# Attention products with v: low part beside the high part, column 0 apart, and two joined block pairs in each head

## The chip, the cores and the metric

The kernel runs on one core of one Trainium2 chip. The time is device microseconds of one execution; 967.84 us is the median of three runs before the change (967.84 to 968.23). The engines are named as in the profile: PE is TensorE (PEld its weight loads), DVE is VectorE, ACT is ScalarE, POOL is GpSimd, SP is SyncE, which here only issues DMAs. Each takes its instructions strictly in the order in which the program issued them to it.

## The reference

Attention in which a query sees the keys of its own hash bucket only, followed by a two-layer feed-forward stage, all in float32:

```
q_bits = (einsum('bhsd,dk->bhsk', q, proj) > 0); k_bits likewise; bucket = sum(bits * 2**k)
scores = where(q_bucket == k_bucket, q k^T / sqrt(64), -1e9)
attn = exp(scores - max); attn /= sum(attn) + 1e-9
x = (attn @ v) laid out as 3072 tokens x 512
h = x @ w_in;  g = (h + 1)^2 / 4 between -1 and 1, h above, 0 below;  out = g @ w_out
```

q, k and v are 4 batches x 8 heads x 768 positions x 64; w_in is 512 x 2048 and w_out 2048 x 512.

## The kernel before

Both stages keep float32 accuracy with TensorE's float32r type, which holds a number with fewer bits: every operand is split into a high part (the rounded number) and a low part (the rest), and a product is the sum of high x high, low x high and high x low.

**Attention** takes about the first 450 us. The 32 heads lie in 16 pairs. A head is cut into 12 units: two halves of 384 queries, and six blocks of 128 keys in each. Unit g (`s_unit`) makes the scores of its block with two matmuls (L421, L422) into one of four PSUM banks `s`; ScalarE takes the exponential twice, once rounded into `ph` (L430) and once in full (L435), back into the bank or, for the units that GpSimd serves, into an SBUF tile `pf`. `lo_unit` of the unit before subtracts the two into `pl` (line 39, the helper `sub`): on GpSimd for blocks 0 and 3 (`POOL_J`), on VectorE for the rest. Four units later (`LAG`), `pv_unit` multiplies with v in three matmuls: `va` x `ph` (L454), `vb` x `ph` (L456) and `va` x `pl` (L458). `va` holds the 64 columns of v's high part and 64 columns of ones, so that the lower or upper half of the 128 output rows collects the sums of the exponentials; `vb` holds v's low part and zeros. The blocks of a half are taken in the order 1, 2, 0, 4, 5, 3 (`PV_ORDER`). After the last, ScalarE copies the bank (L464), and after the second half SP stores the head's result and its sums.

The maxima of head hd + 2 are made meanwhile: after every second unit two matmuls (`max_mm`, L343) fill the one two-bank buffer `smax`, and at the start of the next unit VectorE reduces it (`max_red`, L360). The next two matmuls into `smax` wait for that reduction.

The order of the work is written out by hand. The main loop at the end of `attention` runs over g: scores of unit g, the reduction, `lo_unit(g - 1)`, `pv_unit(g - 4)`, the matmuls for a maximum, and then the tasks entered for that g with `at`. Among these tasks are, for each pair, on even heads: the splitting of the pair after next on GpSimd (`cast_h`, `low_h`), its hash bits (matmuls L219, ScalarE L225, VectorE L230, in units 5 to 8), the cast of the next pair's v on ScalarE (L305, entered for unit 6) and its low part on GpSimd. In most heads, units 9 to 14 carry a share of the conversion of the feed-forward weights from 64-bit words (ScalarE L66, VectorE L70, L74, L78).

**The feed-forward stage** takes the rest. It loads x (the attention result, kept in DRAM as `x_d`), divides it by the sums (`XMaker`) and multiplies with the two weight matrices. GpSimd does nothing in it.

## Time and profile before

| | us |
|---|---|
| median of three runs | 967.84 |
| the profiled execution: span from first to last instruction | 965.5 |
| busy in the span: TensorE, VectorE, ScalarE, GpSimd | 957.1, 752.7, 679.8, 322.7 |
| the pair of heads 18 and 19, from the first scores of one to those of the next | 26.98 |

The span is 2.3 us short of the median; what lies around the first and the last instruction is in the runs' times and not in the span. Matmuls are pipelined, so that the row of one lasts longer than the step from its start to the next start; for a price, the steps are what counts. In the timeline a row gives the start, the duration, engine, line, operation, tiles, shapes and count; in brackets stands how long the engine idled before it and what ended that. Successive operations of VectorE and ScalarE overlap by about a tenth of a microsecond.

### The profile page before, as it was taken

To read this page: it belongs to the slowest core of one execution; us is meant where nothing else is said; L and a number is where in the kernel's file an instruction comes from. 1 tells how busy PE (TensorE), PEld (TensorE's weight loads), DVE (VectorE), ACT (ScalarE), POOL (GpSimd) and SP (SyncE) were. 2 spreads that over 40 slices of the span, in tenths; PEclk is the share of its full clock that TensorE was granted. 3 is DMA by queue.
4 is the path that set the end of the run, shared out by engine and by line. 5 is a ranking of instruction groups with operands and counts; after the bars stand their busy time and mean duration, and the time that the engine had idled before them with its cause. 6 is when DMAs were issued, how large, how long until landed. Compare 5 with 4: busy or idle time off the path is not lost.

```text
span 965.5 us, 15605 instructions
## 1 busy us (share of the span) xinstructions
PE 957.1 (99%) x5050; PEld 889.9 (92%) x5050; DVE 752.7 (78%) x1341; ACT 679.8 (70%) x1481; POOL 322.7 (33%) x435
## 2 busy tenths in 40 slices
...
GB/s 163 189 178 181 164 169 174 183 180 198 202 180 188 158 174 167 148 107 170 186 344 44 200 214 310 308 216 184 120 186 215 156 175 120 147 150 119 121 88 65
DMA packets 95112, 167.55 MB, mean 174 GB/s; under 512 B 13956, under 2 KB 51960, under 8 KB 95032
## 3 DMA queue, kind: packets, MB, share of 16 engines
...
q10 hardware_dynamic: 264, 0.03, 0.0%
...
## 4 chain that ended last, share of the span: by engine, by line
PE 97%; DVE 2%; ACT 1%; issue 0%; DVEq 0%
PE y L893 27%; PE h L1125 18%; PE h L1030 7%; PE s L421 7%; PE o L458 7%; PE o L456 7%; PE o L454 7%; PE s L422 7%; PE smax L343 6%; PE o L219 2%; PE half L343 1%; DVE nm L350 0%; PE half L475 0%; DVE nm L323 0%; PE s L398 0%
## 5 line engine op out<-in xcount | busy, mean ns | idle before, releaser
L430 ACT ACTIVATE ph<-s 128x384 fp32r<-128x384 f32 x380 | 189.8, 500 | 32.1 <-PE s L422 26.1
L360 DVE TENSOR_REDUCE nm<-smax 128x1 f32<-128x768 f32 x168 | 159.9, 952 | 17.5 <-PE smax L343 17.5
L39 DVE TENSOR_TENSOR pl<-s,ph 128x384 fp32r<-128x384 f32 x256 | 137.9, 550 | 26.9 <-ACT s L435 25.6
L39 POOL TENSOR_TENSOR pl<-pf,ph 128x384 fp32r<-128x384 f32 x128 | 129.8, 1014 | 84.3 <-ACT pf L435 79.4
L858 DVE SCALAR_TENSOR_TENSOR t<-t 128x384 f32<-128x384 f32 x128 | 71.3, 557 | 106.7 <-ACT z L853 106.5
L421 PE MATMUL s<-t 128*128 128x384 f32 x384 | 130.5, 340 | 0.0
L454 PE MATMUL o<-ph,va 128*128 128x386 f32 x384 | 130.0, 339 | 0.0
L456 PE MATMUL o<-ph,vb 128*128 128x386 f32 x384 | 130.0, 338 | 0.0
L458 PE MATMUL o<-pl,va 128*128 128x386 f32 x384 | 130.0, 338 | 0.0
L422 PE MATMUL s<-t 128*128 128x384 f32 x384 | 129.4, 337 | 0.0
L435 ACT ACTIVATE s<-s 128x384 f32<-128x384 f32 x252 | 126.2, 501 | 0.0
L893 PE MATMUL y<-t,ghi 128*128 128x512 f32 x384 | 124.6, 395 | 0.0
L852 ACT ACTIVATE t<-h,mh 128x384 f32<-128x384 f32 x56 | 32.5, 581 | 83.7 <-PE h L1030 44.1
L343 PE MATMUL smax<-t 128*128 128x384 f32 x336 | 87.6, 342 | 0.4 <-DVE nm L360 0.3
L863 ACT CAST ghi<-z 128x384 fp32r<-128x384 f32 x129 | 65.2, 505 | 30.1 <-DVE z L859 26.3
L853 ACT ACTIVATE z<-t,m 128x384 f32<-128x384 f32 x128 | 79.0, 617 | 4.2
L893 PEld LDWEIGHTS y<-t,ghi 128*128 128x128 f32 x384 | 71.3, 188 | 11.0 <-ACT ghi L863 0.3
L1125 PE MATMUL h<-wbig,t 128*128 128x384 f32 x399 | 81.4, 336 | 0.0
L852 ACT ACTIVATE t<-wsq,mh 128x384 f32<-128x384 f32 x48 | 29.6, 617 | 67.0 <-DVE wsq L1138 40.8
L1125 PEld LDWEIGHTS h<-wbig,t 128*128 128x128 f32 x399 | 71.6, 188 | 5.2
L893 PE MATMUL y<-t,glo 128*128 128x512 f32 x192 | 76.0, 396 | 0.0
L893 PE MATMUL y<-woh,glo 128*128 128x512 f32 x192 | 75.7, 394 | 0.2
...
## 6 DMA issues: line engine op xcount, KB each, us to landing
...
```

Source lines behind the costliest of these rows:

```text
L39: eng.tensor_tensor(out=out, in0=a, in1=b, op=ALU.subtract)
L343: nc.tensor.matmul(out=ps[:, 0:HS], lhsT=t2[:, 0, h, i * P:(i + 1) * P], rhs=t2[:, 1, h, hf * HS:(hf + 1) * HS], start=True, stop=True)
L360: nc.vector.tensor_reduce(out=nmp(hd)[:, i:i + 1], in_=smax[hd][:, :, 0:HS], axis=AX.XY, op=ALU.max, negate=True)
L421: nc.tensor.matmul(out=ps[:, 0:HS], lhsT=t1[:, 1, h, ks], rhs=t1[:, 0, h, sl], start=True, stop=False)
L422: nc.tensor.matmul(out=ps[:, 0:HS], lhsT=t2[:, 1, h, ks], rhs=t2[:, 0, h, sl], start=False, stop=True)
L430: nc.scalar.activation(out=ph[:, 0:HS], in_=ps[:, 0:HS], func=AF.Exp, scale=SCALE)
L435: nc.scalar.activation(out=pf, in_=ps[:, 0:HS], func=AF.Exp, scale=SCALE)
L454: nc.tensor.matmul(out=o, lhsT=wa, rhs=ph, start=(jj == 0), stop=False)
L456: nc.tensor.matmul(out=o, lhsT=wb, rhs=ph, start=False, stop=False)
L458: nc.tensor.matmul(out=o, lhsT=wa, rhs=pl, start=False, stop=(jj == NJ - 1))
L893: nc.tensor.matmul(out=ys[c][m], lhsT=g_[:, m * P:(m + 1) * P], rhs=w, start=(first and k == 0), stop=(last and k == 2))
L1125: nc.tensor.matmul(out=ps, lhsT=w[:, cs], rhs=x, start=(n == 0 and s not in (2, 3, 6)), stop=(n == 5), skip_group_check=True)
```

## The change

- One tile `VT` replaces `va` and `vb`: for each key block and head 64 columns of v's high part and beside them the low part of columns 1 to 63, with a column of ones in place of the low part's column 0. One matmul with `ph` and one with `pl` then give the high product in rows 0 to 63 and the low product in rows 65 to 127, with the sums in row 64.
- The low part of v's column 0 is left. It has a table of its own, `v0lo`, for all heads, and a matmul of one output row with `ph`, added to row 0. The tables come from a new input `v0` in two loads, and `first_column` makes them: for the first three pairs ahead of the first cast, for the rest at unit 40. `cast_v` gets a second copy that places the high part of column 0.
- From head 4 on (`FROM` = 48) the column-0 products of blocks 4 and 5 of a head's first half (unit 5) and of blocks 0 and 1 of its second half (unit 7) are joined: `z_unit` makes z = ratio x `ph` of the unit before + the full exponential of this unit on VectorE, and one matmul with the later block's `v0lo` serves both. The ratios are made once (`ratios`); `z_ends` sets two columns for each pair from pair 2 on. A joined product is issued up to three units later than the others.
- `QUARTER_J` gives GpSimd one more low part, that of block 1 in the second half of odd heads (from unit 48 to head 29). `pf` gets a third buffer.
- A head's result is stored as two tensors, `x_d` and the low product `l_d`; `add_low` adds the second to the first by accumulating DMAs from GpSimd's queue, two for each batch.
- Products with `pl`, and all products of a first half, are 384 columns wide, not 386. The memsets of `vb` and of the ends of `pl` fall away.

```diff
+FROM = 48
 POOL_J = (0, 3)
+QUARTER_J = ((0, 3), (0, 3), (0, 3), (0, 1, 3))
...
     def cast_v(pr, eng):
-        (eng.copy if eng is nc.scalar else eng.tensor_copy)(out=VA[pr % NV][:, :, 0::2], in_=vraws[pr])
+        copy = eng.copy if eng is nc.scalar else eng.tensor_copy
+        vt = VT[pr % NV]
+        copy(out=vt[:, :, 0::2, 1:], in_=vraws[pr][:, :, :, 1:])
+        copy(out=vt[:, :, 0::2, 0], in_=v0hi[:, pr].bitcast(F32))
...
+    def first_column(a, b, eng):
+
+        n = slice(2 * NJ * a, 2 * NJ * b)
+        hi, lo = (x.rearrange("p a j h -> p (a j h)")[:, n] for x in (v0hi, v0lo))
+        t = v0_raw[:, n]
+        if eng is nc.gpsimd:
+            eng.tensor_scalar(out=hi, in0=t, scalar1=AWAY, scalar2=0.0, op0=ALU.mult, op1=ALU.add)
...
+        sub(nc, eng, t, t, hi.bitcast(F32))
+        eng.tensor_scalar(out=lo, in0=t, scalar1=0.0, scalar2=TINY, op0=ALU.is_equal, op1=ALU.mult)
+        eng.tensor_tensor(out=lo, in0=lo.bitcast(F32), in1=t, op=ALU.add)
...
     def pool_lo(g):
-        return g % NJ in POOL_J
+        return g % NJ in (QUARTER_J[g // NJ % 4] if FROM <= g < (NH - 2) * NU else POOL_J)
...
+    def z_ends(pr):
+
+        nc.vector.tensor_scalar(out=ZT[0][:, :, HS:HS + 2],
+                                in0=ratio[:, pr, 0].rearrange("p (h o) -> p h o", o=1).to_broadcast([P, 2, 2]),
+                                scalar1=1.0, scalar2=None, op0=ALU.add)
+
+    def z_unit(g):
+
+        hd, n = g // NU, g % NJ // 4
+        if g not in zpair:
+            return
+        pa, pb = units[g - 1][1], units[g][0]
+        zs[g] = ZT[n][:, hd % 2]
+        nc.vector.scalar_tensor_tensor(out=zs[g][:, 0:HS], in0=pa[:, 0:HS].bitcast(F32),
+                                       scalar=ratio[:, hd // 2, n, hd % 2:hd % 2 + 1],
+                                       in1=pb, op0=ALU.mult, op1=ALU.add)
...
-        _, ph, pl = units.pop(n - jj + j)
-        o = obank[hf][:, 0:HS + 2]
-        wa = va[:, j, h:h + 2, :].rearrange("p g d -> p (g d)")
-        wb = vb[:, j, h:h + 2, :].rearrange("p g d -> p (g d)")
-        nc.tensor.matmul(out=o, lhsT=wa, rhs=ph, start=(jj == 0), stop=False)
+        vt = VT[pr % NV]
+        g = n - jj + j
+        _, ph, pl = units.pop(g)
+        w = HS if hf == 0 else HS + 2
+        o = obank[hf][:, 0:w]
+        wa = vt[:, j, 2 * h:2 * h + 2].rearrange("p g d -> p (g d)")
+        nc.tensor.matmul(out=o, lhsT=wa, rhs=ph[:, 0:w], start=(jj == 0), stop=False)
         between(3)
-        nc.tensor.matmul(out=o, lhsT=wb, rhs=ph, start=False, stop=False)
+        if g in zpair:
+            late_c.append((3 if jj == 0 else jj + 1, j, zs.pop(g)))
+        elif g + 1 not in zpair:
+            late_c.append((jj, j, ph))
+        for c in [c for c in late_c if c[0] <= jj]:
+            late_c.remove(c)
+            _, jc, x = c
+            nc.tensor.matmul(out=o[0:1], lhsT=v0lo[:, pr, jc, h:h + 1], rhs=x[:, 0:w], start=False, stop=False)
         between(4)
-        nc.tensor.matmul(out=o, lhsT=wa, rhs=pl, start=False, stop=(jj == NJ - 1))
+        nc.tensor.matmul(out=obank[hf][:, 0:HS], lhsT=wa, rhs=pl, start=False, stop=(jj == NJ - 1))
...
-                nc.sync.dma_start(out=x_d[hd // H][rs:rs + 64, pr % (H // 2), :], in_=xs[rs:rs + 64])
-                nc.sync.dma_start(out=s_d[hd // H][hd % H:hd % H + 1, :], in_=xs[sr:sr + 1, 0:S])
+                r = 64 * h
+                nc.sync.dma_start(out=x_d[hd // H][r:r + 64, pr % (H // 2), :], in_=xs[0:64])
+                nc.sync.dma_start(out=l_d[hd // H][r + 1:r + 64, pr % (H // 2), :], in_=xs[65:P])
+                nc.sync.dma_start(out=s_d[hd // H][hd % H:hd % H + 1, :], in_=xs[64:65, 0:S])
...
+    nc.sync.dma_start(out=v0_raw[:, 0:6 * NJ], in_=v0[:, 0:6 * NJ])
     load_v(0)
     load_raw(1)
+    nc.sync.dma_start(out=v0_raw[:, 6 * NJ:], in_=v0[:, 6 * NJ:])
...
+    first_column(0, 3, nc.gpsimd)
     cast_v(0, nc.gpsimd)
...
+    at(40, first_column, 3, NPAIR, nc.gpsimd)
+    at(43, ratios)
...
+        if h == 0 and pr > 1:
+            at(g + 4, z_ends, pr)
...
+    zpair = {g for g in range(FROM, NG) if g % NU in (5, 7)}
...
             lo_unit(g - 1)
+            z_unit(g - 1)
...
+    def add_low(self, b, h):
+
+        r = slice(64 * h + 1, 64 * h + 64)
+        self.nc.gpsimd.dma_start(out=self.x_d[b][r].rearrange("p c s -> p (c s)"),
+                                 in_=self.l_d[b][r].rearrange("p c s -> p (c s)"), accum_op=ALU.add,
+                                 max_dma_last_dim=S * 8)
...
+    for h in range(2):
+        at(N1 + 20 + 4 * h, xm.add_low, B - 1, h)
...
+        for h in range(2):
+            at(g + 11 + 3 * h, xm.add_low, b, h)
```

57 lines of the change are left out of this document (35 added, 22 removed).

## The prediction

> **What bounds the kernel now.** I read the page first, then busy times by stretch, then the timeline of one pair of heads (18 and 19).
>
> ```profile
> span 965.5 us, 15605 instructions
> PE 957.1 (99%) x5050; PEld 889.9 (92%) x5050; DVE 752.7 (78%) x1341; ACT 679.8 (70%) x1481; POOL 322.7 (33%) x435
> 264.51:291.49 26.98, 26.98 (x156) 26.57 (x155) 23.78 (x38) 25.14 (x61) 18.89 (x24) 1.00 0.64 181
> ```
>
> TensorE is never idle in this pair (26.98 us of 26.98), so a matmul taken out looks like time taken out. But VectorE is busy for 23.78 us and ScalarE for 25.14 of the same 26.98, and TensorE waits for VectorE at every maximum: the two matmuls of L343 fill one buffer, which the reduction of L360 has to empty before the next two. How close is that? Below, the starts of three such pairs of matmuls, then VectorE around them. I count units of the pair from 0 to 23 (unit 0 starts at 264.51); the three stand at the ends of units 10, 14 and 22.
>
> ```profile
> 277.48 0.51 PE L343 MATMUL smax<-t 128*128 128x384 f32 x2
> ...
> 281.68 0.55 PE L343 MATMUL smax<-t 128*128 128x384 f32 x2
> ...
> 290.26 0.51 PE L343 MATMUL smax<-t 128*128 128x384 f32 x2
> ```
> ```profile
> 275.08 0.56 DVE L39 TENSOR_TENSOR pl<-s,ph 128x384 fp32r<-128x384 f32 x1 [1.01 <-ACT s L435]
> 275.55 0.53 DVE L230 TENSOR_TENSOR neg<-o,neg 32x384 f32<-32x384 f32 x1
> 276.02 0.93 DVE L360 TENSOR_REDUCE nm<-smax 128x1 f32<-128x768 f32 x1
> 276.88 0.53 DVE L39 TENSOR_TENSOR pl<-s,ph 128x384 fp32r<-128x384 f32 x1
> 277.56 0.69 DVE L70 TENSOR_SCALAR o<-wraw 128x512 int32<-128x512 int32 x1
> 278.17 0.95 DVE L360 TENSOR_REDUCE nm<-smax 128x1 f32<-128x768 f32 x1
> ...
> 280.62 0.95 DVE L360 TENSOR_REDUCE nm<-smax 128x1 f32<-128x768 f32 x1
> ...
> 286.59 0.96 DVE L360 TENSOR_REDUCE nm<-smax 128x1 f32<-128x768 f32 x1 [0.32 <-PE smax L343]
> 287.92 0.56 DVE L39 TENSOR_TENSOR pl<-s,ph 128x384 fp32r<-128x384 f32 x1 [0.37 <-ACT s L435]
> 288.70 0.96 DVE L360 TENSOR_REDUCE nm<-smax 128x1 f32<-128x768 f32 x1 [0.23 <-PE smax L343]
> 289.58 0.55 DVE L39 TENSOR_TENSOR pl<-s,ph 128x384 fp32r<-128x384 f32 x1
> 290.33 0.70 DVE L70 TENSOR_SCALAR o<-wraw 128x512 int32<-128x512 int32 x1 [0.20 <-ACT xs L464]
> ```
>
> The reduction of 276.02 ends at 276.95, and the matmuls that need its buffer start at 277.48: 0.53 us to spare. The one of 280.62 ends at 281.57, its matmuls start at 281.68: 0.11 to spare. From 275.08 to beyond 280.62 no row shows a wait that matters, so work put into VectorE's queue near 275 arrives at 281.68 almost undiminished. TensorE at 100% is here a balance of two engines, not one engine with room beside it.
>
> **The products.** Each key block keeps three matmuls of 384 columns where the old `vb` product becomes the one-row product of column 0; where two blocks are joined it is two. Units 5 and 7 of each head from head 4 on are joined: 28 heads x 2 = 56 matmuls fewer of 1152. Their price, and the only narrow products of this trace:
>
> ```profile
> 285.06 0.22 PE L398 MATMUL s<-ident_r,nmr 128*12 128x128 f32 x1
> 285.12 0.39 PE L421 MATMUL s<-t 128*128 128x384 f32 x1
> 285.35 0.34 PE L422 MATMUL s<-t 128*128 128x384 f32 x1
> ```
>
> The pair's 26.98 us hold 156 matmuls, two of them of 128 columns at 0.06 each (285.06 to 285.12), so a wide one costs 26.86/154 = 0.174. Hence 56 x 0.174 = 9.8 us less. The 12-row product takes 0.06 for a third of 384 columns: time goes with the moving columns, so a one-row product of 384 costs what a full one does, and a gain below that is excluded. The 768 products that shrink from 386 to 384 columns give 768 x 2 x 0.06/128 = 0.7 us. Behind the 12-row product the next matmul took 0.23 (285.12 to 285.35) instead of 0.174; if narrowness causes that, each of the 328 one-row products costs up to 0.055 more. I take 0, because the narrow product here was also short, and so could hide little of the next weight load, which a 384-column one can.
>
> The Trainium skill (TensorEngine Tiling (Array Packing), section Tiling Modes) says that changing the tiling mode drains TensorE, and a product for few output rows would be such a change. The row gives at most 0.055 for it; by the row's zero the sum stays as it is, by the page it is the third rival below.
>
> **The extra ScalarE copy.** `cast_v` gets a second, tiny copy. The cast of v sits in the even head, in an unbroken run of ScalarE work ahead of unit 7's exponentials:
>
> ```profile
> 273.37 0.84 ACT L305 CAST va<-vraw 128x768 fp32r<-128x768 f32 x1
> 274.09 0.51 ACT L430 ACTIVATE ph<-s 128x384 fp32r<-128x384 f32 x1
> 274.47 0.51 ACT L435 ACTIVATE s<-s 128x384 f32<-128x384 f32 x1
> ...
> 285.53 0.25 ACT L403 CAST te<-s 12x128 fp32r<-12x128 f32 x1
> 285.72 0.49 ACT L430 ACTIVATE ph<-s 128x384 fp32r<-128x384 f32 x1
> 286.11 0.49 ACT L435 ACTIVATE pf<-s 128x384 f32<-128x384 f32 x1
> 286.94 0.49 ACT L430 ACTIVATE ph<-s 128x384 fp32r<-128x384 f32 x1 [0.34 <-PE s L422]
> 287.33 0.49 ACT L435 ACTIVATE s<-s 128x384 f32<-128x384 f32 x1
> ```
>
> The nearest small copy (285.53) holds the next one up by 0.19. So unit 7's second exponential, and VectorE's row of 275.08 which waits for it, come 0.19 later.
>
> **The joins on VectorE.** `z_unit` adds one operation with a scalar per partition, 128x384. The same form with VectorE undisturbed:
>
> ```profile
> L770 DVE SCALAR_TENSOR_TENSOR pcs<-t,xsva,pcs 128x384 f32<-128x384 f32 x4 | 2.5, 613 | 0.0
> ```
>
> Successive operations overlap by about 0.09 (275.08 + 0.56 against 275.55), so one costs the queue 0.52. *Even head.* Unit 5's join falls into an idle stretch ahead of the first comparison and costs nothing; if that were full it would add 0.52 to what follows. Unit 7's comes right behind the row of 275.08, and pushes the comparison, the reductions and the low parts behind it. Reduction 276.02 moves by 0.19 + 0.52 to 276.73 and ends at 277.66, 0.18 after the matmuls of 277.48 started, which TensorE, with two products fewer by then, would have liked 0.35 earlier. The wait of L70 (0.15 between 277.41 and 277.56) takes back 0.2, so reduction 280.62 ends at about 282.07: TensorE passes 281.68 some 0.40 later than before, instead of 0.35 earlier.
>
> *Odd head.* TensorE gains its 0.35 there, VectorE idles 0.32, 0.37 and 0.23 in the rows from 286.59 on, and unit 17's join mostly disappears in them: 0.05 behind the old time. But `QUARTER_J` moves the low part of unit 19 (row 287.92) to GpSimd, so its exponential goes to SBUF, and this join reads two operands from SBUF while GpSimd works on the same two. What that does is shown later in the trace, where the same operation meets a GpSimd subtraction:
>
> ```profile
> 428.33 1.27 DVE L770 SCALAR_TENSOR_TENSOR raw<-t,xsv,raw 128x384 f32<-128x384 f32 x1
> ```
> ```profile
> 428.17 1.01 POOL L39 TENSOR_TENSOR t<-raw,t 128x384 fp32r<-128x384 f32 x1
> ```
>
> The join's form takes 1.27 instead of 0.613 and ends 0.42 after GpSimd's (429.60 against 429.18): it waited it out. Which starts first here? Both wait for the same exponential.
>
> ```profile
> 286.67 1.01 POOL L39 TENSOR_TENSOR pl<-pf,ph 128x384 fp32r<-128x384 f32 x1 [1.62 <-ACT pf L435]
> ```
>
> GpSimd starts 0.07 after it (286.60 to 286.67), VectorE 0.10 (287.82 to 287.92). So GpSimd first: it runs 287.89 to 288.90, the join ends at 289.32, with the 0.40 at 289.72; the reduction that stood at 288.70 then starts at 289.64 and ends at 290.60, while its matmuls stood at 290.26. L70's wait of 0.20 takes some back, about 0.6 stays in VectorE's queue up to the next place with 0.11 to spare. I take +0.49 per pair (0.60 less that 0.11). Bounds: +0.05 if VectorE goes first, +0.75 if nothing is taken back.
>
> **DMA and the rest.** Per head SP issues one more store; per batch GpSimd issues two accumulating DMAs, which the trace does not contain. The nearest row is a long issue on SP:
>
> ```profile
> 280.56 1.23 SPq L62 DMA_DIRECT2D wraw<-in_w_in_dram  x1
> ```
>
> They stand at units 7 and 10 of an odd head, the first just ahead of unit 19's low part, which thereby comes later, so that the join goes first; I take half of 0.49 for these three pairs, between 0.05 and 0.49 + 2 x 1.23. The fourth batch's are issued in the second stage, where GpSimd has nothing else. Two small loads and four small GpSimd operations at the start are ahead of work not yet due: 0, at most one issue, 1.23. `ratios` and `z_ends` are tiny and run where VectorE waits: 0. With the cover gone, `z_ends` could wait out a GpSimd operation, 1.01, ahead of a reduction with over 1 us to spare.
>
> **Sum.** Heads 4 to 29 are 13 pairs with maxima: 10 x 0.49 + 3 x 0.25 = +5.65. Heads 30 and 31 have none, there the four products come out whole: -0.70. Together +4.95; the profiled 965.5 becomes 970.5, and the median, 2.3 above the span, 967.84 becomes 972.8.
>
> **The rivals.** (1) VectorE gets the operands first in the odd heads, or the conflict does not arise: 13 x 0.05 - 0.70, 967.8, no change. For: 0.03 us decide. Against: the two start times. (2) VectorE's added work in the even head stays hidden and TensorE sets the pace: 967.84 - 9.8 - 0.7 = 957.3. For: TensorE is busy everywhere, and VectorE idles 1.01 right ahead of 275.08. Against: that idle time lies before the join's operand exists. It decides at 0.18 us: up to there (0.53 to spare less the 0.35 by which TensorE is early) added delay costs nothing; between 0.18 and the 0.71 I reckon with, part of the gain is left. (3) The one-row products drain TensorE: 0.055 x 20 per pair, of which the even half hides behind VectorE's delay: 0.55 x 13 + 0.055 x 48 in heads 0 to 3 = +9.8 on the forecast, 982.6. (4) The accumulating DMAs hold GpSimd for several us and the low parts behind them stop TensorE: 3 x 2 x 1.23 more gives 980.
>
> **Numbers.** Forecast 45%; (1) 20%; (2) with its partial forms 25%; (3) 5%; (4) 5%. A change under 0.2% (1.9 us) cannot be told from none. Faster: (2) and a little of (1), 0.27; same: most of (1) and a sliver of the forecast, 0.22; slower 0.51. The range must take in (2) at 957.3 and, above, the forecast with its pairs at 0.75 (13 x 0.26 = 3.4 more) and one issue: 977. By itself the forecast runs from 969 to 977.
>
> **What would show it.** In the changed profile: L343 of units 10, 14 and 22 with idle time ended by VectorE's reduction, some 0.5 us a pair, where there was none; unit 7's join at about 0.61 in even heads and 1.4 in odd ones; matmuls with one output row 0.17 apart. The even-head step is wrong if TensorE still shows no idle time in heads 4 to 29; the odd-head step if both joins last 0.61; the price of the products if a one-row product is followed by a longer step than 0.174.

## The result, and the profile after

The changed kernel takes 981.89 us (median of four runs, 979.84 to 982.82) against 967.84 us: slower by a ratio of 1.0143, with a 95% interval of 1.0129 to 1.0157. The forecast was slower, 972.8 us, and its range ended at 977.0. The direction held, the size did not: +14.05 us where +4.95 stood.

The page of the changed kernel, its span, its busy times and the queue that is new:

```profile
span 980.3 us, 15836 instructions
...
PE 959.7 (98%) x4994; PEld 848.2 (87%) x4994; DVE 781.0 (80%) x1402; ACT 678.6 (69%) x1496; POOL 350.7 (36%) x457
...
q0 software_dynamic: 1536, 6.21, 3.5%
```

TensorE has 56 instructions fewer, as counted, and yet is busy for 2.6 us more; weight loads fell by 42 us, and VectorE and GpSimd work 28 us more each. The span grew by 14.75 us (980.3 against 965.55 in unrounded times). To see where, I cut both traces at the first score product of each even head and at the first product of the feed-forward stage:

| stretch | before, us | after, us | difference | forecast |
|---|---|---|---|---|
| up to the end of pair 0 (heads 0, 1) | 45.29 | 45.46 | +0.17 | 0 |
| pair 1 | 30.08 | 31.82 | +1.74 | 0 |
| pairs 2, 3, 5, 6, 7, 9, 10, 11, 13 (ordinary) | 27.19, then 26.94 to 26.98 | 27.19, then 27.03 to 27.17 | +1.04 together | +0.49 each, 4.41 |
| pairs 4, 8, 12 (accumulating DMAs) | 27.04, 27.05, 27.02 | 28.45, 28.27, 28.27 | +3.88 together | +0.25 each, 0.75 |
| pair 14 (heads 28, 29) | 25.72 | 27.10 | +1.38 | +0.49 |
| heads 30, 31 | 24.33 | 24.43 | +0.10 | -0.70 |
| feed-forward stage | 516.12 | 522.55 | +6.43 | 0 |

The part that the forecast worked out most closely, the ordinary pair, lost 0.12 us on average and not 0.49. Nearly all the rest lies where it had put nothing or little.

**An ordinary pair.** Heads 18 and 19 again; unit 0 now starts at 269.51. Busy times of the pair in one row (columns: stretch, its length and TensorE's busy time, then weight loads, VectorE, ScalarE, GpSimd, granted clock, DMA share, GB/s):

```profile
269.51:296.68 27.17, 26.92 (x152) 23.85 (x151) 25.18 (x42) 24.74 (x61) 20.85 (x27) 1.00 0.88 239
```

Four matmuls fewer, and TensorE now idles for 0.25 us of the pair, where it did not before. (The count in brackets takes in matmuls that only reach into the stretch: 154 start in the pair before, 150 now.) In the timeline of TensorE:

```profile
281.00 0.34 PE L519 MATMUL o<-z,v0lo 128*1 128x384 f32 x1
281.18 0.34 PE L519 MATMUL o<-ph,v0lo 128*1 128x384 f32 x1
281.35 0.34 PE L521 MATMUL o<-pl,vt 128*128 128x384 f32 x1
...
282.17 0.34 PE L521 MATMUL o<-pl,vt 128*128 128x384 f32 x1
282.76 0.62 PE L378 MATMUL smax<-t 128*128 128x384 f32 x2 [0.25 <-DVE nm L395]
...
287.14 0.62 PE L378 MATMUL smax<-t 128*128 128x384 f32 x2
...
295.44 0.52 PE L378 MATMUL smax<-t 128*128 128x384 f32 x2
```

One-row products follow each other at 0.18 and 0.17 us. The maxima's products at the ends of units 10, 14 and 22 stand 13.25, 17.63 and 25.93 us into the pair, where they stood at 12.97, 17.17 and 25.75: 0.28, 0.46 and 0.18 late. At unit 10 TensorE stops (282.17 to 282.76 for a step of 0.17). What VectorE did:

```profile
280.31 0.56 DVE L42 TENSOR_TENSOR pl<-s,ph 128x384 fp32r<-128x384 f32 x1 [1.13 <-ACT s L470]
280.78 0.60 DVE L494 SCALAR_TENSOR_TENSOR z<-ph,ratio,s 128x384 fp32r<-128x384 f32 x1
281.30 0.54 DVE L239 TENSOR_TENSOR neg<-o,neg 32x384 f32<-32x384 f32 x1
281.77 0.94 DVE L395 TENSOR_REDUCE nm<-smax 128x1 f32<-128x768 f32 x1
...
293.45 0.62 DVE L494 SCALAR_TENSOR_TENSOR z<-ph,ratio,pf 128x384 fp32r<-128x384 f32 x1 [0.26 <-ACT pf L470]
```

The join of unit 7 (280.78) pushes the reduction; VectorE had idled 1.13 us ahead of it, waiting for ScalarE. In the odd head the join of two SBUF operands (293.45) lasts 0.62 us and not 1.4. GpSimd at the same time:

```profile
293.55 1.40 POOL L42 TENSOR_TENSOR pl<-pf,ph 128x384 fp32r<-128x384 f32 x1 [0.32 <-POOL pl L42]
```

GpSimd came 0.10 us after VectorE, and it was GpSimd that waited (1.40 against its usual 1.02). Of the 13 such joins the group's row gives least, median and most in ns:

```profile
L494 DVE SCALAR_TENSOR_TENSOR z<-ph,ratio,pf x13: 618/620/2068, 101.2 to 429.3; 128x384 fp32r<-128x384 f32 x13
```

**Pair 4.** The longest of them, VectorE first and then GpSimd:

```profile
151.63 0.94 DVE L805 TENSOR_SCALAR sm<-sm 128x48 f32<-128x48 f32 x1
...
155.68 2.07 DVE L494 SCALAR_TENSOR_TENSOR z<-ph,ratio,pf 128x384 fp32r<-128x384 f32 x1
```
```profile
155.11 1.15 POOL L819 DMA_DIRECT2D xd<-ld  x1
156.01 1.32 POOL L42 TENSOR_TENSOR pl<-pf,ph 128x384 fp32r<-128x384 f32 x1
```

The join starts while GpSimd issues the accumulating DMA and ends 0.42 us after the low part behind it (157.75 against 157.33): it waited out both. TensorE then waits for the reductions before and after it:

```profile
155.81 0.62 PE L378 MATMUL smax<-t 128*128 128x384 f32 x2 [0.30 <-DVE nm L395]
158.67 0.62 PE L378 MATMUL smax<-t 128*128 128x384 f32 x2 [0.50 <-DVE nm L395]
```

**Pair 1.** ScalarE's cast waits for v, and some 18 us later TensorE waits for a reduction that stands behind `ratios` in VectorE's queue (its first and last operation, then TensorE):

```profile
56.81 0.83 ACT L316 CAST vt<-vraw 128x756 fp32r<-128x756 f32 x1 [1.89 <-DMA vraw<-in_v_dram]
```
```profile
72.91 0.34 DVE L340 RECIPROCAL ratio<-v0lo 128x32 f32<-128x32 f32 x1
...
74.00 0.20 DVE L343 TENSOR_SCALAR ratio<-ratio 128x64 f32<-128x64 f32 x1
```
```profile
75.58 0.62 PE L378 MATMUL smax<-t 128*128 128x384 f32 x2 [0.32 <-DVE nm L395]
```

**The feed-forward stage.** Its first products start at 457.75. TensorE stops twice:

```profile
463.42 4.44 PE L1104 MATMUL h<-t,wbig 128*128 128x384 f32 x24 [1.35 <-ACT t L926]
...
476.75 3.93 PE L1104 MATMUL h<-t,wbig 128*128 128x384 f32 x12 [2.51 <-ACT t L926]
```

The first stop: ScalarE's first operation of the stage has to wait for the last head's stores and what stands behind them. The second: ScalarE waits 5.48 us for weights in a cast that stands ahead of its activation.

```profile
462.79 0.58 ACT L926 ACTIVATE t<-h,mh 128x384 f32<-128x384 f32 x1 [3.32 <-DMA xsva<-xd]
...
475.19 0.62 ACT L87 CAST t<-wsq 128x512 fp32r<-128x512 f32 x1 [5.48 <-DMA wsq<-wd]
```

The chain of waits names the load, and GpSimd's queue shows what moved beside it:

```profile
462.92 12.25 DMA wsq<-wd
```
```profile
461.51 1.00 POOL L819 DMA_DIRECT2D xd<-ld  x1
463.01 0.88 POOL L819 DMA_DIRECT2D xd<-ld  x1 [0.51 <-issue]
```

The fourth batch's accumulating DMAs were entered for steps some 170 us into the stage (run 6, which makes them wait for a tile of that time, issues them 166 and 173 us in). GpSimd has nothing in its queue ahead of them there and no reason to wait, so they go out as soon as the last head is stored, into the stretch in which the stage loads its first operands. The row of the DMA issues gives a median of 11.0 us from issue to landing (9.6 for the first, 12.4 for the second):

```profile
xd<-ld POOLq DMA_DIRECT2D x2, 758.0 KB, 11.0
```

And the 12 products after the second stop take 3.93 us, 0.32 each, where 24 took 4.44: another 1.7 us. By stretch the granted clock there was

```profile
461.50:480.20 18.70, 14.84 (x69) 13.19 (x68) 10.81 (x21) 9.76 (x19) 1.89 (x3) 0.91 0.91 241
```

0.91. (1.69 - 0.18) + (2.91 - 0.24) + 1.7 = 5.9 of the 6.4 us, where 1.69 and 2.91 are the steps over the two stops, from start to start. The slow products do not come every time: of the six traces with these DMAs in this place (the changed kernel and runs 3, 4, 5, 7, 13) all have the second stop, a step of 2.3 to 2.9 us, but three have the slow products behind it. With them the stage took 522.44 to 522.55 us, without 520.38 to 520.97.

### The profile page after: what moved, and what is told of

Read it like the earlier page. It is cut to its first block, busy times and chain, and to the rows that moved or that the text cites. A ratio compares the mean times of both kernels' runs of the same rounds, so it can differ in the third digit from the quotient of the medians.

```text
span 980.3 us, 15836 instructions
## 1 busy us (share of the span) xinstructions
PE 959.7 (98%) x4994; PEld 848.2 (87%) x4994; DVE 781.0 (80%) x1402; ACT 678.6 (69%) x1496; POOL 350.7 (36%) x457
## 4 chain that ended last, share of the span: by engine, by line
PE 81%; DVE 7%; ACT 5%; DMA 3%; issue 2%; POOL 1%; SPq 0%; ACTq 0%; DVEq 0%; POOLq 0%
PE y L967 26%; PE h L1201 18%; PE h L1104 6%; PE smax L378 5%; PE s L457 5%; PE s L456 5%; PE o L521 5%; PE o L510 5%; PE o L519 4%; DVE nm L395 2%; ACT ph L465 1%; PE o L228 1%; DMA wsq<-wd 1%; DVE pl L42 1%; ACT s L470 1%
## 5 line engine op out<-in xcount | busy, mean ns | idle before, releaser
L42 POOL TENSOR_TENSOR pl<-pf,ph 128x384 fp32r<-128x384 f32 x141 | 149.0, 1057 | 64.0 <-ACT pf L470 55.0
L42 DVE TENSOR_TENSOR pl<-s,ph 128x384 fp32r<-128x384 f32 x243 | 129.6, 545 | 23.3 <-ACT s L470 21.3
L510 PE MATMUL o<-ph,vt 128*128 128x386 f32 (+1 forms) x384 | 130.9, 341 | 0.7 <-DVE neg L239 0.7
L521 PE MATMUL o<-pl,vt 128*128 128x384 f32 x384 | 130.4, 339 | 0.2
L470 ACT ACTIVATE s<-s 128x384 f32<-128x384 f32 x239 | 120.4, 504 | 0.0
L378 PE MATMUL smax<-t 128*128 128x384 f32 x336 | 91.3, 353 | 6.7 <-DVE nm L395 6.5
L521 PEld LDWEIGHTS o<-pl,vt 128*128 128x128 f32 x384 | 72.5, 189 | 26.4 <-DVE pl L42 1.2
L519 PE MATMUL o<-ph,v0lo 128*1 128x386 f32 (+1 forms) x272 | 92.2, 339 | 0.0
```

The costliest lines, as they stand in the source:

```text
L42: eng.tensor_tensor(out=out, in0=a, in1=b, op=ALU.subtract)
L378: nc.tensor.matmul(out=ps[:, 0:HS], lhsT=t2[:, 0, h, i * P:(i + 1) * P], rhs=t2[:, 1, h, hf * HS:(hf + 1) * HS], start=True, stop=True)
L470: nc.scalar.activation(out=pf, in_=ps[:, 0:HS], func=AF.Exp, scale=SCALE)
L510: nc.tensor.matmul(out=o, lhsT=wa, rhs=ph[:, 0:w], start=(jj == 0), stop=False)
L519: nc.tensor.matmul(out=o[0:1], lhsT=v0lo[:, pr, jc, h:h + 1], rhs=x[:, 0:w], start=False, stop=False)
L521: nc.tensor.matmul(out=obank[hf][:, 0:HS], lhsT=wa, rhs=pl, start=False, stop=(jj == NJ - 1))
```

## The experiments

Theories at the outset: (A) the losses have separate places and causes: the fourth batch's DMAs, the joins where they meet GpSimd's DMA issues, the join of unit 7. (B) The forecast's own: every pair pays for the conflict of its odd-head join. (C) The form in two matmuls costs time by itself. All stretches, in us, cut as above (ordinary: median of pairs 3, 5, 6, 7, 9, 10, 11, 13):

| kernel | time | pair 1 | ordinary | pairs 4, 8, 12 | pair 14 | feed-forward |
|---|---|---|---|---|---|---|
| before | 967.84 | 30.08 | 26.97 | 27.04, 27.05, 27.02 | 25.72 | 516.12 |
| after | 981.89 | 31.82 | 27.08 | 28.45, 28.27, 28.27 | 27.10 | 522.55 |
| 1 no fourth add | 977.31 | 31.34 | 27.08 | 28.46, 28.32, 28.30 | 27.13 | 518.22 |
| 2 no add | 975.15 | 30.64 | 27.09 | 27.70, 27.71, 27.71 | 27.21 | 517.82 |
| 3 no join | 977.54 | 32.20 | 27.14 | 27.13, 27.40, 27.36 | 25.75 | 520.97 |
| 4 no join in unit 7, even | 979.14 | 31.72 | 26.83 | 28.18, 28.00, 28.12 | 27.30 | 522.44 |
| 5 no third low part | 980.65 | 30.70 | 27.32 | 27.79, 27.78, 27.75 | 27.70 | 520.65 |
| 6 adds moved | 999.23 | 30.66 | 30.18 | 27.72, 27.74, 27.73 | 32.79 | 519.19 |
| 7 cast on GpSimd | 982.07 | 31.47 | 26.96 | 27.16, 26.99, 27.93 | 27.22 | 522.45 |
| 8 all edits | 989.16 | 32.29 | 27.09 | 28.04, 27.92, 28.04 | 27.15 | 519.36 |
| 9 split add | 970.34 | 31.47 | 26.42 | 27.14, 27.15, 28.08 | 26.39 | 516.91 |
| 10 fewer joins | 971.50 | 31.21 | 26.87 | 27.20, 27.22, 27.43 | 26.39 | 516.92 |
| 11 quarters | 971.65 | 30.93 | 26.42 | 28.08, 28.05, 28.02 | 25.79 | 517.39 |
| 12 before, cast on GpSimd | 967.68 | 30.10 | 26.95 | 27.03, 27.05, 26.99 | 25.73 | 516.36 |
| 13 sums on GpSimd | 980.77 | 31.29 | 27.09 | 29.96, 27.16, 28.30 | 27.13 | 520.38 |
| 14 causes taken away | 967.19 | 31.52 | 26.46 | 26.94, 26.91, 26.94 | 25.72 | 519.58 |
| 15 two more edits | 969.32 | 29.98 | 26.43 | 26.95, 26.91, 30.80 | 25.75 | 516.51 |
| 16 third batch spread | 964.48 | 30.56 | 26.42 | 26.93, 26.98, 26.93 | 25.73 | 516.45 |

### One suspect at a time

**1, without the fourth batch's DMAs.**

```diff
-    for h in range(2):
-        at(N1 + 20 + 4 * h, xm.add_low, B - 1, h)
```

> The changed kernel without the two accumulating DMAs of the fourth batch (its low product is left out of the result; nothing else changes). Theory: these two DMAs, issued by GpSimd at 461.5 and 463.0 us, hold back the loads of the feed-forward stage and stop TensorE twice; the stage falls from 522.5 us back to 516 to 517 us and the time from 981.9 to about 975.6 us. Rival: the feed-forward stage is longer because attention ends differently (later stores, other clock); then it stays at 521 to 523 us and the time within 0.7 us of 981.9.

The stage fell by 4.33 us and the second stop is gone, with the slow products behind it; against the three traces without slow products it is 2.2 to 2.8 us. The time, 977.31, is 1.7 above the theory's. The first stop stayed (a step of 1.69 us, and 1.67 in run 2), so the stage is 1.7 to 2.1 us above before: that part has another cause (run 9).

**2, without any of these DMAs.**

```diff
-        for h in range(2):
-            at(g + 11 + 3 * h, xm.add_low, b, h)
```

> The changed kernel without any of the eight accumulating DMAs (all low products but those of column 0 are left out of the result). Theory: beside the feed-forward stage they cost 1.2 to 1.4 us in each of the three pairs of heads 8/9, 16/17, 24/25, which fall from 28.3 to 27.1 us, so that the time is about 971.8 us. Rival: these three pairs are slow for another reason that falls on the same heads (the sums' loads and the reciprocal, in the kernel before too); then they stay at 28.3 us and the time equals that of the run without the fourth batch's DMAs.

Halfway between theory and rival: 28.3 became 27.70, not 27.1, and the time 975.15. The DMAs are half of the loss in pairs 4, 8 and 12. VectorE in pair 4 without them, then GpSimd:

```profile
154.40 1.32 DVE L494 SCALAR_TENSOR_TENSOR z<-ph,ratio,pf 128x384 fp32r<-128x384 f32 x1
```
```profile
154.28 1.02 POOL L42 TENSOR_TENSOR pl<-pf,ph 128x384 fp32r<-128x384 f32 x1 [0.38 <-POOL pl L42]
```

VectorE's queue is late in these pairs, so GpSimd is first, 0.12 us ahead; the join lasts 1.32 us and ends 0.42 after GpSimd. That is the forecast's mechanism with the forecast's price, in the pairs for which it had been denied.

The Trainium skill (SBUF — State Buffer, section SBUF: two separate sides) says that whichever of the two starts first holds the shared pair of ports for its whole instruction, and that the other is blocked. The trace agrees in both orders: 0.62 us for the join that starts 0.10 ahead, 1.32 for the one that starts 0.12 behind. Recorded starts that lie closer than that do not tell the order (run 14).

**4, without the join of unit 7 in even heads.**

```diff
-    zpair = {g for g in range(FROM, NG) if g % NU in (5, 7)}
+    zpair = {g for g in range(FROM, NG) if g % NU in (5, 7) and g % (2 * NU) != 7}
```

> The changed kernel without the join in unit 7 of the even heads (two one-row products take its place, as in heads 0 to 3; same result). Theory: this join makes the reduction in unit 10 late and so costs TensorE 0.4 us there and 0.1 us at unit 14, against 0.18 us for the one-row product that it saves; an ordinary pair falls from 27.10 to about 26.8 us, the time by 3 to 4.5 us to 977.4 to 978.9. Rival: the stop in unit 10 comes from the second copy of the cast on ScalarE; then it stays, and the pair gains 0.18 us to 27.3, the time 984.

26.83: the theory (the time, 979.14, is 0.2 above its range). A join that saves one product of 0.17 us cost 0.25 more than it saved.

**5, without the third low part on GpSimd.**

```diff
-QUARTER_J = ((0, 3), (0, 3), (0, 3), (0, 1, 3))
+QUARTER_J = ((0, 3), (0, 3), (0, 3), (0, 3))
```

> The changed kernel with the low part of block 1 in the second half of odd heads on VectorE again (same result). Forecast's theory: the join that reads two SBUF tiles meets GpSimd's low part there and one waits for the other; with it gone an ordinary pair falls by 0.3 to 0.5 us. Rival, from the trace of the changed kernel (VectorE goes first and the join takes 0.62 us): ordinary pairs do not fall and may grow by up to 0.4 us, as VectorE does half a microsecond more. In both, if the sharing of SBUF between the two engines is what makes heads 9, 17 and 25 and heads 28/29 slow, these pairs fall by 1.0 to 1.4 us each, to 27.0 to 27.4 and 25.7 us; if it is the accumulating DMAs' traffic, they stay at 28.3 us.

Ordinary pairs rose by 0.24: theory (B) falls. Pairs 4, 8 and 12 fell by 0.5 to 0.66; with one operand in PSUM the join there takes 0.60. Pair 14 rose, so it is not this low part alone that slows it (without joins it costs the pair 0.64 us, runs 9 and 10 against run 3).

**3, without joins and third low part.**

```diff
-QUARTER_J = ((0, 3), (0, 3), (0, 3), (0, 1, 3))
+QUARTER_J = ((0, 3), (0, 3), (0, 3), (0, 3))
...
+    zpair = set()
```

> The changed kernel without any join and without the extra low part on GpSimd (every column-0 product is a matmul of its own, 154 matmuls in a pair as before; same result). Theory: without joins a pair has TensorE's time of before, 26.97 to 27.05 us, since a one-row product takes the same 0.175 us as the product that it replaces; pairs 4, 8 and 12 lose the joins' share of their delay and come to 27.3 to 27.8 us, pair 14 to 25.7 to 26.0 us; the feed-forward stage stays at 522 us; time 976 to 978 us. Rival: the two-matmul form itself (second copy in the cast, third store, narrower products) delays a pair; then it stays at 27.1 us or above without the joins and the time at 980 us or above.

The ordinary pair stays at 27.1: all joins together bring an ordinary pair nothing, and the form in two matmuls costs it 0.1 to 0.2 us (theory (C), in small; which part of it, the second copy in the cast or the stores, no run tells). Pairs 4, 8 and 12, with their DMAs, come to 27.1 to 27.4, and pair 14 to 25.75. So the DMAs alone cost little there: it takes a join that waits for GpSimd. In pair 14 the joins do it in another way. VectorE in the changed kernel:

```profile
426.63 0.61 DVE L494 SCALAR_TENSOR_TENSOR z<-ph,ratio,s 128x384 fp32r<-128x384 f32 x1
427.15 1.40 DVE L847 TENSOR_TENSOR raw<-raw,t 128x384 f32<-128x384 f32 x1
428.48 0.94 DVE L395 TENSOR_REDUCE nm<-smax 128x1 f32<-128x768 f32 x1
```

and without joins:

```profile
424.33 0.55 DVE L847 TENSOR_TENSOR raw<-raw,t 128x384 f32<-128x384 f32 x1
```

The join pushes an operation on x (L847, two SBUF operands, which heads 28 and 29 have in addition) behind the start of a low part on GpSimd; it lasts 1.40 instead of 0.55. With the join's 0.52 the reduction comes 1.4 us late.

### Moving the causes away

**6, the DMAs moved and delayed.**

```diff
-            at(g + 11 + 3 * h, xm.add_low, b, h)
+            at(g + 9 + 2 * NU * h, xm.add_low, b, h)
...
+        at(N1 + 20 + 4 * h, lambda h=h: nc.gpsimd.tensor_copy(out=mark[:, h:h + 1], in_=pc[h][:, 0:1]))
         at(N1 + 20 + 4 * h, xm.add_low, B - 1, h)
...
+    zpair = {g for g in range(FROM, (NH - 4) * NU) if g % NU in (5, 7)}
```

> The changed kernel with three edits in stretches that do not touch each other (same result): the accumulating DMAs of the first three batches issued in unit 5 of heads 9 and 11, 17 and 19, 25 and 27, when GpSimd has no low part due; those of the fourth batch behind a small copy on GpSimd that needs a tile of step N1+18; no joins in heads 28 and 29. Theory: in pairs 4, 8, 12 it is GpSimd's time to issue the DMA, put ahead of a low part, that makes the join wait, and not the traffic; they fall from 28.3 to 27.7 us as without the DMAs, pairs 5, 9, 13 stay at 27.1; the feed-forward stage falls from 522.5 to 518 us, since there the traffic only hurts while the first operands are loaded; pair 14 falls from 27.1 to 25.7 to 26.0; time about 974 us. Rivals: the traffic itself delays the pairs (4, 8, 12 stay at 28 and 5, 9, 13 rise by half a microsecond); the stops of the feed-forward stage come again 180 us later (stage 521 us or more); pair 14 is slow for the third store (stays at 27).

The theory was wrong, by 25 us. Pairs 4, 8 and 12 did fall to 27.7, but the pairs that follow a head with such a DMA rose by 2.5 to 5.8 us, pair 14 among them, in which nothing can be told of the joins for that reason. TensorE at the start of a pair:

```profile
187.79 0.34 PE L456 MATMUL s<-t 128*128 128x384 f32 x1
190.31 0.62 PE L457 MATMUL s<-t 128*128 128x384 f32 x1 [2.18 <-DMA t<-te]
...
191.37 0.84 PE L378 MATMUL smax<-t 128*128 128x384 f32 x2
192.01 0.52 PE L456 MATMUL s<-t 128*128 128x384 f32 x1
192.33 0.52 PE L457 MATMUL s<-t 128*128 128x384 f32 x1
```

The load `t<-te`, a row that the scores of the next head need, was issued by SP 0.81 us after GpSimd began to issue the accumulating DMA, and landed 7.8 us later (182.46 to about 190.3):

```profile
182.46 1.40 SPq L440 DMA_DIRECT2D t<-te  x1
```
```profile
181.65 0.95 POOL L819 DMA_DIRECT2D xd<-ld  x1
```

So the traffic does cost, by whom it delays. The delayed DMAs of the fourth batch took the feed-forward stage to 519.19, not 518: other stops, 192 and 195 us into the stage. Behind the stop of 2.5 us the products step at 0.32 us (191.37 to 192.01 for two, 192.01 to 192.33).

**7, the cast of v on GpSimd.**

```diff
-            gv = g + LAG + (2 if pr else 16)
-            at(gv, cast_v, pr + 1, nc.scalar)
+            late_v = 0 < pr < NPAIR - 2
+            gv = g + LAG + (10 if late_v else 2 if pr else 16)
+            at(gv, cast_v, pr + 1, nc.gpsimd if late_v else nc.scalar)
```

> The changed kernel with one edit from pair 1 to pair 13: the cast of the next pair's v, two copies of 1.04 us together on ScalarE in unit 6 of the even head, is done by GpSimd in unit 2 of the odd head, and the low parts of v eight units later too (same result). Theory: the cast makes ScalarE late in units 6 to 8, so that VectorE stands idle for 0.84 us of unit 8 and has no room for the join of unit 7 before the reduction that TensorE needs in unit 10; without it VectorE starts earlier, the stop of 0.41 us goes, and an ordinary pair falls from 27.10 to 26.4 to 26.6 us; time about 975 us. Rival: VectorE has too much work over units 9 to 15 whatever happens before; then the pair stays at 27.0 to 27.1, or grows where GpSimd's casts meet the joins that read SBUF.

The stop of unit 10 is gone, but a stop of 0.41 us came up at unit 22: with the cast and v's low parts ahead of it, GpSimd now is done with its operation before at about the moment at which the odd-head join starts, takes the low part 0.04 us after it and not 0.10, and the join lasted 1.49 us. The time, 982.07, stayed. Where GpSimd comes first in an ordinary pair, the forecast's +0.4 does appear. Pairs 5 and 9 stopped for 2.7 and 1.8 us at the start of their odd heads, in the manner of run 6.

**8, all these edits.**

```diff
+                (nc.sync if hd < NH - 1 else nc.scalar).dma_start(out=l_d[hd // H][r + 1:r + 64, pr % (H // 2), :], in_=xs[65:P])
...
+                at(gv + (6 if pr else 3), load_v, pr + 2)
```

> All edits together (same result): the accumulating DMAs moved and delayed, no joins in heads 28 and 29, the cast of v on GpSimd in the odd head, the second load of v one unit earlier, and the low product of the last head stored over ScalarE's queue instead of behind the other store on SP's. Theory: what was found adds up: ordinary pairs 26.4 to 26.6 us, pairs 4, 8, 12 0.5 us above them, pair 14 25.7 to 26.0, the feed-forward stage 516.1 to 516.6 us as before, pair 1 30.1 to 30.7; time 962 to 966 us, below the kernel before. Rival: VectorE's work bounds the pairs at 27.0 us; then the time is 968 to 971 us.

989.16 us: the DMAs' place of run 6 hurt here too, now by GpSimd's queue. The issue, a low part of v and three low parts stand there in a row, the odd-head joins of pairs 5, 9 and 13 last 3.4 to 3.9 us, and TensorE stops for 2.7, 2.7 and 2.2 us in unit 22 for the reductions behind them. Pair 1, with its load of v a unit earlier, took 32.29.

**9, cast two units earlier, DMAs of the fourth batch in quarters.**

```diff
+            late_v = 1 < pr < NPAIR - 2
+            gv = g + LAG + (8 if late_v else 2 if pr else 16)
...
+    zpair = {g for g in range(FROM, (NH - 4) * NU) if g % NU in (5, 7) and g // (2 * NU) % 4}
...
+    for ct in range(NCT):
+        n = N1 + 20 + 4 * ct
+        at(n, lambda ct=ct: nc.gpsimd.tensor_copy(out=mark[:, ct:ct + 1], in_=pc[ct][:, 0:1]))
+        for h in range(2):
+            at(n, xm.add_low, B - 1, h, ct)
```

> The changed kernel with five edits, read stretch by stretch (same result): (a) the cast of v on GpSimd again, but in unit 0 of the odd head and only for pairs 2 to 13, its low parts one and three units later; (b) no joins in pairs 4, 8, 12 and 14; (c) the fourth batch's low product added in eight DMAs of a quarter of the size, two behind each of four small copies on GpSimd that need a tile of steps N1+15 to N1+25; (d) the last head's low product stored over ScalarE's queue; (e) the ratios one unit later. Theory: (a) with GpSimd's backlog gone before the low parts of units 18 and 19, the stop does not move to unit 22, and an ordinary pair falls to 26.4 to 26.6 us; (b) pairs 4, 8, 12 come to 27.1 to 27.4 and pair 14 to 25.7; (c, d) small DMAs leave room for the weight loads between them and the first ScalarE operation of the stage no longer waits for three stores in one queue: 516.1 to 516.8 us; (e) pair 1 loses 0.3 to 0.5 us; time 963 to 967 us. Rivals: VectorE's work over units 9 to 15 keeps the ordinary pair at 26.9 us; any accumulating DMA holds the weight loads up, and the stage stays at 518 to 519 us; then 969 to 971 us.

The ordinary pair is 26.42, 0.55 below before: now the four products come out of TensorE's time almost whole (0.70). The feed-forward stage is 516.91; its first stop went from a step of 1.69 to 0.76 us with the last low product stored over another queue, and the quarters delay nobody. Left over: pair 5 at 31.25 and pair 9 at 27.88, where the two whole DMAs of a batch still ran ahead of `t<-te` (the profiled execution, 973.47, is 3 us longer than the five others). With the ratios a unit later, TensorE's stop at the end of pair 1 stayed (a step of 0.65). The time, 970.34, is above the 963 to 967 expected. Pair 14 is at 26.39 without joins, and run 3, also without the third low part, had 25.75.

**10, the cast on ScalarE, no join of unit 7 in even heads** (the diff is against run 9).

```diff
-            late_v = 1 < pr < NPAIR - 2
...
+    zpair = {g for g in range(FROM, (NH - 4) * NU) if g % NU in (5, 7) and g // (2 * NU) % 4 and g % (2 * NU) != 7}
```

> As the kernel before it in this list with (b) to (e), but the cast of v on ScalarE where it was, and no join in unit 7 of even heads. Theory: an ordinary pair 26.8 us as with that join left out alone; the other stretches as there: 27.1 to 27.4 for pairs 4, 8, 12, 25.7 for pair 14, 516.1 to 516.8 for the feed-forward stage; time 967 to 969 us, no more than even with the kernel before. Rival as there for the feed-forward stage: 969 to 971 us.

Pairs as expected (26.87, but pair 5 at 27.59 with a stop for `t<-te`; 27.2 to 27.4), the stage 516.92; the time, 971.50, is above the expectation for pair 1 (31.21) and pair 14 (26.39).

**11, every DMA in quarters.**

```diff
-        for h in range(2):
-            at(g + 11 + 3 * h, xm.add_low, b, h)
+        for q in range(8 if b < 2 else 0):
+            at(g + 4 + 2 * NU * (q // 2) + 2 * (q % 2), xm.add_low, b, q % 2, q // 2)
```

> The changed kernel (same result) with the cast of v on GpSimd in unit 0 of the odd head for pairs 1 to 13, the joins kept in pairs 4, 8 and 12 but not in heads 28 and 29, which also lose the extra low part on GpSimd, the last head's low product stored over ScalarE's queue, the tables of column 0 one and two units later, and every accumulating DMA cut into quarters: for the first two batches one quarter in units 0 and 2 of each odd head of the following pairs, for the third and the fourth in the feed-forward stage behind small copies on GpSimd. Theory: a 0.8 MB accumulating DMA holds back the small load of a row that the scores of the next head need, which cost 3.4 us at the start of the odd head of pair 5 and 1.5 us in pair 9 when the casts ran on GpSimd; in quarters this stop is gone, every ordinary pair comes to 26.4 to 26.5 us, pairs 4, 8, 12 to 26.4 to 26.9, pair 14 to 25.75, the feed-forward stage to 516.5 to 517.5; time 961 to 965 us, faster than the kernel before by 0.3 to 0.7%. Rival: any accumulating DMA, of a quarter too, delays the loads that fall on it; then pairs 4 to 11 stay at 27 us or above and the time at 967 to 971 us.

Quarters are free in the ordinary pairs: 26.42 in each, no stop at an odd head's start. But with their joins back, pairs 4, 8 and 12 stand at 28.0 with no DMA being issued then: the sums' two small operations are enough to make VectorE late, the join of 1.32 us and its stops return, as in run 2. Pair 2 is at 28.70, with a stop of 2.1 us at its start: the reduction that TensorE waits for starts at 77.63, behind the five operations of `ratios`, which take 2.7 us in their later place (74.96 to 77.70, two of them 0.84 and 1.00 beside GpSimd's) against 1.3 in the changed kernel. The time, 971.65, is not the 961 to 965 expected.

**12, the kernel before with the cast on GpSimd.**

```diff
+            late_v = 1 < pr < NPAIR - 2
+            gv = g + LAG + (8 if late_v else 2 if pr else 16)
+            at(gv, cast_v, pr + 1, nc.gpsimd if late_v else nc.scalar)
```

> The kernel before, with the cast of v on GpSimd in unit 0 of the odd head for pairs 2 to 13 and nothing else (same result). Theory: in the kernel before, ScalarE's lateness in units 6 to 8 costs TensorE only 0.05 to 0.1 us in a pair, because VectorE has no join to put in; an ordinary pair falls from 26.96 to 26.85 to 26.95 us, the time to 966 to 967.8 us, so that the shorter pair of the changed kernel with this edit is the joins' doing. Rival: the move of the cast is worth 0.5 us in a pair by itself; then the time is 961 to 963 us.

967.68, ratio 0.9999 (0.9990 to 1.0009): the move alone is worth nothing. It is worth 0.65 us a pair only to a kernel that has joins.

**13, the sums' small operations on GpSimd.**

```diff
-        at(g + 7, xm.sums_add)
+        at(g + 9, xm.sums_add, nc.gpsimd)
```

> The changed kernel with one edit (same result): the two small operations on the sums of the exponentials (128x48) in pairs 4, 8 and 12 run on GpSimd, two units later, not on VectorE. Theory: VectorE's queue is full there, and these two take 1.1 us of it, 0.7 of that in waiting for GpSimd's low part; without them the joins of units 17 and 19 start a microsecond earlier and TensorE's two stops of 0.46 and 0.66 us go for the larger part: the three pairs fall from 28.3 to 27.3 to 27.5 us, the time by 2.5 to 3 us. Rival: the wait of the second join for GpSimd, which issues the accumulating DMA ahead of its low part, makes the delay; then only the first stop goes and the pairs stay at 27.8 to 27.9 us, the time falls by 1.2 to 1.5 us.

Neither. Pair 8 came down to 27.16, pair 12 stayed at 28.30 and pair 4 rose to 29.96. The joins tell why: with VectorE a microsecond earlier, the join now meets another point of GpSimd's queue. In pair 8 it slipped through in 0.62 us; in pair 4, VectorE and GpSimd:

```profile
154.50 3.33 DVE L494 SCALAR_TENSOR_TENSOR z<-ph,ratio,pf 128x384 fp32r<-128x384 f32 x1 [0.26 <-ACT pf L470]
```
```profile
154.24 1.14 POOL L823 DMA_DIRECT2D xd<-ld  x1
155.14 2.28 POOL L42 TENSOR_TENSOR pl<-pf,ph 128x384 fp32r<-128x384 f32 x2
```

It waited for the issue of the DMA and then for two low parts queued behind it. Of the six joins in this kernel and the changed one that started while GpSimd issued such a DMA, five waited 1.0 to 2.7 us; over all traces it is 12 of 13.

**14, every cause named so far taken away.** Runs 9, 11 and 13 together: the cast early on GpSimd, quarters, the sums on GpSimd, no joins and no third low part in heads 28 and 29, the last low product over ScalarE's queue.

```diff
+        return g % NJ in (QUARTER_J[g // NJ % 4] if FROM <= g < (NH - 4) * NU else POOL_J)
...
+        n = (16, 20, 28, 31)[ct]
+        at(n, lambda ct=ct: nc.gpsimd.tensor_copy(out=mark[:, ct:ct + 1], in_=pc[ct][:, 0:1]))
+        for h in range(2):
+            at(n, xm.add_low, B - 2, h, ct)
```

> The changed kernel with every named cause taken away (same result): the cast of v on GpSimd in unit 0 of the odd head for pairs 2 to 13; the accumulating DMAs in quarters, as in the run with the quarters before; the sums' small operations on GpSimd; no joins and no extra low part on GpSimd in heads 28 and 29; the last head's low product stored over ScalarE's queue. Theory: ordinary pairs 26.4 us, pairs 4, 8, 12 26.4 to 26.9, pair 14 25.8, pairs 0 and 1 together 63.5 to 64.5, the feed-forward stage 516.9 to 517.4; time 963.5 to 966 us, 0.2 to 0.45% faster than the kernel before. Rival: a cause not yet named keeps pairs 4, 8 and 12 at 27.2 us or above; then 966.5 to 968 us, no faster than before.

The attention pairs came as expected, but for pair 10 (27.22, with a stop for `t<-te`), the feed-forward stage did not: 519.58, with steps of 0.74 and 2.04 us some 20 and 35 us behind the quarters of steps 28 and 31. That these cause them is not shown: run 11 had quarters at the same steps and 517.39. Even with the kernel before: 0.9999 (0.9990 to 1.0008).

Pairs 4, 8 and 12 stay 0.5 us above the others, and their odd-head join is the reason. It and GpSimd's low part wait for the same exponential (it ends at 152.61 in pair 4). VectorE, then GpSimd:

```profile
152.65 1.48 DVE L494 SCALAR_TENSOR_TENSOR z<-ph,ratio,pf 128x384 fp32r<-128x384 f32 x1 [0.26 <-ACT pf L470]
```
```profile
152.69 1.02 POOL L42 TENSOR_TENSOR pl<-pf,ph 128x384 fp32r<-128x384 f32 x1 [0.22 <-ACT pf L470]
```

The join's recorded start is 0.04 us ahead, and yet it is the join that waits. Over all traces, the 107 odd-head joins that start 0.10 us ahead of GpSimd's low part last 0.62 us; the 23 that start 0.04 to 0.06 ahead last 1.48 or 1.49. So the recorded starts do not give the order when they lie within a tenth of a microsecond. Nor does it follow from GpSimd being free: its low part before had ended 0.19 to 0.24 us ahead of the join's start in the 107, and between 0.21 us ahead and 0.10 us behind in the 23. What decides is open.

**15, the third batch back into attention, v's load on GpSimd's queue.**

```diff
+        (nc.gpsimd if pr == 2 else nc.sync).dma_start(out=vraws[pr], in_=v[pr])
...
+            n, k = (q // 2, 2 * (q % 2)) if b < 2 else (q // 4, 2 * (q % 4))
+            at(g + 4 + 2 * NU * n + k, xm.add_low, b, q % 2, q // 2)
```

> As the last kernel with every named cause taken away, with two more edits (same result): the third batch's low product is added in quarters in units 0, 2, 4 and 6 of heads 25 and 27 and not in the feed-forward stage; the load of v for pair 2 is issued by GpSimd right behind the last use of its buffer, and not by SP behind seven other DMAs. Theory: the feed-forward stage falls from 519.6 to 516.9 us, as in the two runs that had only the fourth batch's quarters there; ScalarE's cast at 56 us no longer waits, and pair 1 falls from 31.5 to 30.1 to 30.7 us; pairs 12 and 13 stay below 27.0; time 963 to 965.5 us, 0.25 to 0.5% faster than the kernel before. Rivals: the stage's stops come from the weight loads' own timing in that run and stay (519 us); a GpSimd DMA of this size lands no earlier (pair 1 stays at 31 us or above); with both the time stays at 967 us.

The stage 516.51 and pair 1 29.98, as the theory said; but pairs 12 and 13, with four issues of about 0.85 us in seven units each, rose to 30.80 and 29.15: in pair 12 TensorE waits 0.53 us for a low part of GpSimd and 2.25 for a reduction behind a join that lasts 4.28. The time, 969.32, missed the theory.

**16, two of the four elsewhere** (the diff is against run 15).

```diff
-        for q in range(8):
-            n, k = (q // 2, 2 * (q % 2)) if b < 2 else (q // 4, 2 * (q % 4))
+        for q in range(8 if b < 2 else 4):
...
+    for ct in (2, 3):
+        n = 8 + 4 * ct
```

> As the last kernel, but of the third batch's eight quarters only two each in heads 25 and 27 (units 0 and 2, as in the other batches) and the other four in steps 16 and 20 of the feed-forward stage, behind small copies on GpSimd (same result). Theory: four DMAs of 0.8 us in six units fill GpSimd's queue, so that its low parts come late; with two the pairs 12 and 13 fall from 30.8 and 29.2 to 26.9 and 26.45 us; four quarters early in the feed-forward stage are free (516.5 to 517.0 us); the span is 960.5 to 961.5 us, the time 962.5 to 964 us, 0.4 to 0.55% faster than the kernel before. Rival: what happened in pairs 12 and 13 was the DMA traffic on other loads, not GpSimd; then the pairs stay above 28 us, or the feed-forward stage rises to 518 us or more, and the time stays at 966 to 969 us.

964.48 us, ratio 0.9968 (0.9956 to 0.9979): 0.3% faster than the kernel before, and half a microsecond above the 962.5 to 964 expected. Its page, and the busy times of its pair 3 in one row, as for the changed kernel above:

```profile
span 961.6 us, 15868 instructions
```
```profile
102.21:128.62 26.41, 26.41 (x151) 23.88 (x151) 25.27 (x41) 24.29 (x60) 21.28 (x28) 1.00 0.71 199
```

TensorE is never idle in it, as in the kernel before, but with four matmuls fewer (150 start in it). The edits put the change's own work in other places; what they take out are the eight joins of heads 28 to 31 (the bound in the diff of run 6 ends there), whose column-0 products are made singly again.

## Why the prediction was wrong, step by step

- **The price of the products** was right: steps of 0.17 to 0.18 us behind one-row products; the third rival, a drain at each of them, did not come. The Trainium skill's sentence on draining at a change of tiling mode (TensorEngine Tiling (Array Packing), Tiling Modes) is not borne out by these steps; whether a product of one row changes the mode at all, no run shows. A slip of the sum: 154 matmuls start in the pair, not 156, so a wide one costs 26.86/152 = 0.177 and the 56 come to 9.9 us instead of 9.8.
- **The even head** was right: 0.28 and 0.46 us late at units 10 and 14, where 0.18 and 0.40 stood; run 4 shows the join as the cause, runs 7 and 9 that it is ScalarE's cast ahead of it that leaves VectorE no time.
- **The odd head failed at "GpSimd starts 0.07 after it [...] VectorE 0.10 [...] So GpSimd first".** The order was read from two start times 0.03 us apart, of other operations. In an ordinary pair GpSimd comes from another low part (its row in the changed kernel names that, not ScalarE, as the end of its wait), VectorE starts 0.10 ahead and GpSimd waits. The term was 0.12 instead of 0.49, the first rival in the ordinary pairs. The price itself was right: wherever GpSimd came first (runs 2, 7, 11, 14), the join took 1.3 to 1.5 us. In 23 joins of runs 7, 8 and 14 to 16 it did come first behind the same exponential, as the forecast had it; what decides between the two outcomes stays open.
- **"The first just ahead of unit 19's low part, which thereby comes later, so that the join goes first"** failed, and with it the 0.25 of pairs 4, 8 and 12 (measured 1.29). The issue of the DMA holds the join up as a low part does, and the low part behind it goes first; besides, VectorE is late there for the sums' operations. The bound written beside it, 0.49 + 2 x 1.23, held the truth; the value taken was at the wrong end.
- **"The fourth batch's are issued in the second stage, where GpSimd has nothing else"** was the costliest sentence: 4.3 us (run 1), of which 1.7 are the slow products that came in three of six traces. An engine with nothing else in its queue is one on which an instruction runs early, not when its step comes. The place in the program was taken for a time. That the two DMAs would be a load on the same 16 engines for 14 us (461.51 to the second's landing, 12.4 after 463.01) was left out: only the issue was priced.
- **"Per head SP issues one more store"** was counted and priced at nothing. In the last head it stands between TensorE's last product and the first operation of the next stage: the first stop, 1.5 us (run 9 took 0.9 of it away by another queue).
- **"`ratios` [...] run where VectorE waits: 0"** and the start at 0: the five operations of `ratios` stand 1.3 us in VectorE's queue ahead of a reduction, and TensorE waits about 0.5 us (one unit later too, run 9). The larger rest of pair 1 is the load of v, which by way of SP's queue came 1.3 us later than before in the changed kernel's trace. Over all traces of changed kernels that load v there for a cast in unit 6, pair 1 took 30.64 to 32.20 us; with the load on GpSimd's queue 29.98 (run 15) and 30.56 (run 16). Why SP comes later in some executions than in others is open.
- **Heads 28 and 29** were counted as an ordinary pair. They have x to make on VectorE and GpSimd, with two SBUF operands, and the joins push that into GpSimd's low parts: 1.38, not 0.49. Runs 3, 11 and 14 show it.
- **Heads 30 and 31**: the 0.70 did not come (+0.10). With joins they took 24.26 to 24.78 us in six traces (24.71 in run 4, with three of four), without 24.48 to 25.09 in nine; the cause was not followed up.

By size: ordinary pairs 3.4 too high, the feed-forward stage 6.4 too low, pairs 4, 8, 12 3.1, pair 1 1.7, pair 14 0.9, heads 30 and 31 0.8 too low, pair 0 0.2: -3.4 + 13.1 = 9.7, against 9.8 measured (14.75 less 4.95). The fourth rival, DMAs that hold GpSimd and stop TensorE, came nearest with 980, and had 5%; its mechanism holds for the 3.9 us of pairs 4, 8 and 12, but that its number fits the whole is luck, for the 6.4 us of the feed-forward stage come by another way. That the direction held is luck too: the term that was to make the kernel slower gave 1.0 us in nine pairs, and what made it slower are terms that the forecast had put at nothing or little.
